# Halved state and score matmuls in a fused linear-attention and MLP kernel

## The chip, the cores and the metric

The kernel runs on one core of a Trainium2 chip. The metric is the device time of one execution in microseconds (us). The engines are named as the profile names them: PE is TensorE's matmuls and PEld its weight loads, DVE is VectorE, ACT is ScalarE, POOL is GpSimd, SP is the engine whose queue issues most loads.

## The reference

Linear attention with a decay per head, and then an MLP with a snake activation on its output. Shapes: batch 4, 8 heads, 768 positions, head size 64; the MLP goes from 512 to 2048 and back to 512 over 3072 tokens.

```python
for b in range(nb):                          # blocks of 64 positions
    intra = einsum('bhic,bhjc->bhij', qb, kb) * Dmask
    intra = einsum('bhij,bhjd->bhid', intra, vb)
    inter = einsum('bhid,bhde->bhie', qb * lam_pow, kv_state)
    out[:, :, sl] = intra + inter
    kv_state = lam_block * kv_state + einsum('bhsd,bhse->bhde', kb * rev_pow, vb)
x = out.transpose(0, 2, 1, 3).reshape(B * S, H * D)
h = x @ w_in
s = sin(alpha * h)
g = h + s * s / (alpha + 1e-9)
return g @ w_out
```

Inputs and the output are float32; the kernel multiplies in bfloat16 and accumulates in float32.

## The kernel before

The attention works on 24 blocks of 128 positions (4 sequences of 6 blocks each). The decay is put into q and k by a scaling on POOL, so that a block needs four kinds of small matmuls, each with 64 or 128 columns of moving data:

- `part_S` (line 535): the scores of a block, 128 keys by 128 queries, for eight heads. Heads lie two to a column group on partitions 0 to 63 and 64 to 127. Eight matmuls contract over 64 partitions into 128 output partitions (one bank of PSUM for the even heads, one for the odd ones). DVE then multiplies by the causal mask into `Sm`.
- `inter` inside `part_O` (line 601): the state's part of the output for the blocks after number 12 that are not first in their sequence (`wide`). `Zd` holds two heads' states of 64 by 64 as blocks on the diagonal of a tile of 128 by 128, so that one matmul serves two heads; four matmuls do it.
- the rest of `part_O` (line 610): for earlier blocks (`n and not wide`) the state's part as eight matmuls of 64 by 64 with `Zc`, and for all blocks eight matmuls of `v2` with `Sm` (line 623), with 64 output partitions each.
- `part_Z` (line 559): the state's update, eight matmuls with 64 output partitions (line 568).

`run` (line 514) puts such parts into one uninterrupted run of matmuls: first every `inter`, then the parts in the order given. `piece_G(s, t)` is the run of the scores of block s, the output of block t and the state update of block t, where t is mostly s - 1. Only the run's last matmul signals the other engines.

The MLP works on six chunks of 512 tokens. `unit_A` and `unit_A2` (lines 671 and 705) are the first product, followed by sin on ACT, a square on ACT or POOL, and a multiply-add on DVE into `gT`; `unit_B` (line 736) is the second product, and ACT copies its result out (line 749). All of these use the array as one tile of 128 by 128. Chunks 2 to 5 run in a loop that puts one unit_A, sometimes a `piece_G`, and one quarter of a unit_B in turn. So most runs of small matmuls stand between two groups of 128 by 128 matmuls.

The order on every engine comes from a planner (`_Plan`): each operation is given an estimated duration, and the planner lays the operations out by these and sets the semaphores. For the runs, the estimates are numbers in the code: 0.33 for `part_S`, and 0.55 for `part_O` where it is wide.

Of the kernel before, what the change touches and what calls it, by code (L numbers as in the profile page):

```python
# [32 lines left out]
class _Plan:  # L33
# [20 lines left out]
    def op(self, eng, emit, dur, reads=(), writes=(), dma=None, after=(), issue=0.4, lat=2.6, runs=64):  # L54
        o = _Op(eng, emit, dur, tuple(reads), tuple(writes), dma, after, issue, lat, runs)
        for b in o.reads:
            if b in self.writer:
                o.deps.add(self.writer[b])
        for b in o.writes:
            if b in self.writer:  # L60
                o.deps.add(self.writer[b])
            o.deps.update(self.readers.get(b, ()))
        o.deps.update(after)
        for b in o.reads:
            self.readers.setdefault(b, []).append(o)
        for b in o.writes:
            self.writer[b] = o
            self.readers[b] = []
        o.deps.discard(o)
        o.lead = self.lead  # L70
        self.ops.append(o)
        return o
# [171 lines left out]
def bass_lightning_attn__then__act_snake_kernel(  # L244
# [35 lines left out]
    with es:  # L280

        def sb(name, shape, dt):
            return es.enter_context(nc.sbuf_tensor(name, shape, dt))

        def ring(name, n, shape, dt):
            return [sb(f"{name}_{i}", shape, dt) for i in range(n)]
# [17 lines left out]
        qkT = sb("qkT", [128, RT, 8, 128], BF16)  # L304
        Sm = ring("Sm", 2, [128, 8, 128], BF16)
        Zc = ring("Zc", 2, [128, 4, D], BF16)
        Zd = ring("Zd", 2, [128, 4, 128], BF16)
# [17 lines left out]
        ps = [banks[:, 512 * i:512 * i + 512] for i in range(8)]  # L325
# [4 lines left out]
        def _(_unused_eng):  # L330
# [7 lines left out]
            def bank(i):  # L338
                return ("bank", i)
# [195 lines left out]
            def part_S(s, b0, b1):  # L535
                jt, jq, u = s % RT, s % RT // 2 * 2, slice(64 * (s % 2), 64 * (s % 2) + 64)

                def mm(e):
                    ins = None
                    for jp in range(4):  # L540
                        for h in range(2):
                            r = slice(64 * h, 64 * h + 64)
                            ins = e.matmul(  # L543
                                ps[(b0, b1)[h]][:, 128 * jp:128 * (jp + 1)].rearrange("p (t x) -> p t x", x=64),
                                qkT[r, jt, 4 + jp, :], qkT[r, jq:jq + 2, jp, u],
                            )
                    return ins

                assert b1 == b0 + 1

                def then():
                    op("DVE", lambda e: e.tensor_tensor(  # L552
                        Sm[s % 2][:, :, :],
                        banks[:, 512 * b0:512 * b0 + 1024].rearrange("p (c i) -> p c i", i=128),
                        mask[:, :, :], ALU.mult), 1.25, [bank(b0), bank(b1), "mask"], [("Sm", s % 2)])

                return mm, 0.33, [("qT", jq), ("qT", jq + 1), ("kT", jt)], [bank(b0), bank(b1)], then
# [31 lines left out]
            def part_O(s, ob, ob2=None):  # L589
                n, j, jq, u = s % NB, s % R2, s % RT // 2 * 2, slice(64 * (s % 2), 64 * (s % 2) + 64)  # L590
                c, i4 = s // BPC, s % BPC
                obs = [ob, ob] if ob2 is None else [ob, ob2]
                new = (0,) if ob2 is None else (0, 2)
                reads = [("v2", j), ("qT", jq), ("qT", jq + 1), ("Sm", s % 2)]
                wide = n and s > SD
                if wide:
                    reads += [("Zd", (s - 1) % 2, 0), ("Zd", (s - 1) % 2, 1)]
                elif n:
                    reads += [("Zc", (s - 1) % 2)]

                def inter(e):
                    for jp in range(4):
                        ins = e.matmul(  # L603
                            ps[obs[jp // 2]][:, 128 * jp:128 * (jp + 1)].rearrange("p (t x) -> p t x", x=64),
                            Zd[(s - 1) % 2][:, jp, :], qkT[:, jq:jq + 2, jp, u],
                            start=(jp in new), stop=False, skip_group_check=True,
                        )
                    return ins

                def mm(e):  # L610
                    ins = None
                    if n and not wide:
                        for jp in range(4):
                            for h in range(2):
                                r = slice(64 * h, 64 * h + 64)
                                e.matmul(
                                    ps[obs[jp // 2]][r, 128 * jp:128 * (jp + 1)].rearrange("p (t x) -> p t x", x=64),
                                    Zc[(s - 1) % 2][r, jp, :], qkT[r, jq:jq + 2, jp, u],
                                    start=(jp in new), stop=False, skip_group_check=True,
                                )  # L620
                    for jp in range(4):
                        for h in range(2):
                            ins = e.matmul(  # L623
                                ps[obs[jp // 2]][64 * h:64 * h + 64, 128 * jp:128 * (jp + 1)],
                                v2[j][:, 2 * jp + h, :], Sm[s % 2][:, 4 * h + jp, :],
                                start=(n == 0 and jp in new), stop=(jp == 3), skip_group_check=True,
                            )
                    return ins

                def then():  # L630
                  for eng, a0, a1, dur in ((("ACT", 0, 2, 0.45), ("DVE", 2, 4, 0.4)) if ob2 is not None else (((("ACT", 0.73, 0.4), ("DVE", 0.7, 0.0)), 0, 4, 0),)):
                    op(eng, lambda e, a0=a0, a1=a1: (e.copy if e is nc.scalar else e.tensor_copy)(  # L632
                        xT[c % RX][:, a0:a1, BL * i4:BL * (i4 + 1)].rearrange("p a (x t) -> p a t x", t=2),
                        ps[obs[a0 // 2]][:, 128 * a0:128 * a1].rearrange("p (a t x) -> p a t x", t=2, x=64)), dur,
                       [bank(obs[a0 // 2])], [("xT", c % RX, i4, a) for a in range(a0, a1)])

                return mm, (0.55 if wide else 0.68) if n else 0.35, reads, [bank(b) for b in sorted(set(obs))], then, inter if wide else None
# [194 lines left out]
            for i in range(NM):  # L832
                hb = (6, 0, 3, 1, 2, 5)[i % 6] if i < 10 else (3, 0, 1, 2)[i % 4]
                u = unit_A2(0, i // 2 * 2, i % 2, hb) if i < 2 else unit_A(0, i, hb)
# [23 lines left out]
            for i in range(8):  # L858
                unit_A2(1, 2 * i, 1, (5, 6, 4)[(i + 2) % 3])
                for _ in range(2 if i in (0, 4) else 1):  # L860
                    kind, s = pieces.pop(0)
# [68 lines left out]
```

## Time and profile before

| | us |
|---|---|
| median of 3 runs | 223.14 |
| lowest and highest | 222.13, 223.40 |
| the profiled execution's own time | 223.52 |
| its span, first to last instruction | 221.4 |
| PE busy in the span | 208.6 (94%), 1645 matmuls |
| ACT, DVE, POOL busy | 155.9, 122.6, 89.1 |

| small matmuls | tile rows*columns | moving columns | count |
|---|---|---|---|
| scores, line 543 | 64*128 | 128 | 192 |
| wide state part, line 603 | 128*128 | 128 | 40 |
| early state part, line 616 | 64*64 | 128 | 80 |
| weighted values, line 623 | 128*64 | 128 | 192 |
| state update, line 568 | 128*64 | 64 | 160 |

Busy time of PE is taken from modelled ends of matmuls that overlap; the starts are recorded one by one, so this text works with starts. A row of the timeline merges the instructions of one line: its first number is the start of the first, its second the stretch to the modelled end of the last. The granted TensorE clock is 1.000 over the span.

### The profile page before, as it was taken

How to read it: one execution, taken by the hardware profiler on the slowest of the kernel's cores; microseconds unless marked ns; L12 is line 12 of the kernel's file. 1: busy time of each engine (PE TensorE's matmuls, PEld its weight loads, DVE VectorE, ACT ScalarE, POOL GpSimd, SP SyncE). 2: the span in 40 equal slices, each digit the busy share in tenths (PEclk: the TensorE clock that was granted, in tenths of full speed). 3: DMA queues.
4: the chain of work that ended last, by engine and by line, in shares of the span. 5: the costliest groups of instructions: out<-in, count | busy, mean ns of one | idle time of the engine just before them, and what ended most of it. 6: DMA issues, size and time to landing. Idle time of an engine off the chain costs nothing.

```text
span 221.4 us, 4062 instructions
## 1 busy us (share of the span) xinstructions
PE 208.6 (94%) x1645; PEld 110.7 (50%) x1645; DVE 122.6 (55%) x184; ACT 155.9 (70%) x277; POOL 89.1 (40%) x100
## 2 busy tenths in 40 slices
PE   3889987899898999999999999999999999999995
PEld 1446433456575785545445444545545444444444
DVE  4687775354777887667655455645465544445100
ACT  3735994347697997788788887877788677778211
POOL 4386763454978776863576103011001011110100
DMA  5999999999999999999999752110110011101112
GB/s 131 236 232 271 206 214 208 217 235 237 233 245 275 242 191 245 219 254 189 276 240 245 155 112 33 47 50 0 47 50 21 26 47 50 47 0 49 75 70 95
DMA packets 83651, 33.31 MB, mean 150 GB/s; under 512 B 63520, under 2 KB 80688, under 8 KB 83632
## 3 DMA queue, kind: packets, MB, share of 16 engines
q1 hardware_dynamic: 76880, 24.25, 53.6%
q0 software_dynamic: 3696, 3.67, 9.9%
q10 hardware_dynamic: 3056, 5.13, 6.4%
q8 instruction: 13, 0.21, 0.4%
q14 instruction: 6, 0.05, 0.1%
HBM read 27.28 MB, written 6.29 MB: 152 GB/s over the span
## 4 chain that ended last, share of the span: by engine, by line
PE 63%; DMA 24%; POOL 4%; SPq 4%; ACT 2%; DVE 1%; issue 1%
PE bank L736 32%; PE bank L671 24%; DMA k<-in_k_dram 10%; DMA q<-in_q_dram 5%; DMA v<-in_v_dram 4%; DMA w<-in_moe_w_in_dram 4%; SPq L342 4%; PE bank L705 3%; PE bank L623 2%; PE bank L543 2%; POOL qk L471 1%; POOL qk L464 1%; PE bank L603 1%; POOL u L720 1%; DVE gT L723 1%
## 5 line engine op out<-in xcount | busy, mean ns | idle before, releaser
L736 PE MATMUL bank<-w,gT 128*128 128x512 bf16 (+1 forms) x400 | 94.8, 371 | 0.0
L688 DVE SCALAR_TENSOR_TENSOR gT<-u,rinv,bank 128x512 bf16<-128x512 bf16 x74 | 54.6, 746 | 51.7 <-ACT u L685 34.2
L671 PE MATMUL bank<-xT,w 128*128 128x512 bf16 x296 | 74.2, 379 | 0.6 <-DVE gT L688 0.6
L681 ACT ACTIVATE t<-bank,alpha 128x512 bf16<-128x512 f32 x74 | 50.6, 686 | 24.1 <-PE bank L671 24.0
L736 PEld LDWEIGHTS bank<-w,gT 128*128 128x128 bf16 x400 | 37.7, 98 | 39.6
L686 POOL TENSOR_TENSOR u<-t 128x512 bf16<-128x512 bf16 x19 | 19.7, 1040 | 80.7 <-ACT t L681 79.7
L671 PEld LDWEIGHTS bank<-xT,w 128*128 128x128 bf16 x296 | 28.5, 98 | 34.9 <-DVE gT L688 1.1
L685 ACT ACTIVATE u<-t 128x512 bf16<-128x512 bf16 x55 | 34.4, 629 | 1.8 <-DVE gT L723 0.3
L552 DVE TENSOR_TENSOR Sm<-bank,mask 128x1024 bf16<-128x1024 f32 x24 | 29.2, 1222 | 10.3 <-PE bank L568 7.7
L464 POOL TENSOR_TENSOR qk<-q,Lq 128x512 bf16<-128x512 f32 x24 | 24.5, 1044 | 21.7 <-DMA q<-in_q_dram 18.1
L471 POOL TENSOR_TENSOR qk<-k,Lk 128x512 bf16<-128x512 f32 x22 | 22.9, 1044 | 7.2 <-DMA k<-in_k_dram 7.0
L749 ACT COPY osb<-bank 128x512 f32<-128x512 f32 (+1 forms) x25 | 14.2, 569 | 14.8 <-PE bank L736 14.8
L705 PE MATMUL bank<-xT,w 128*128 128x256 bf16 x176 | 22.3, 273 | 2.0 <-DVE gT L723 2.0
L723 DVE SCALAR_TENSOR_TENSOR gT<-u,rinv,bank 128x256 bf16<-128x256 bf16 x44 | 19.1, 476 | 7.2 <-POOL u L720 4.1
L715 ACT ACTIVATE t<-bank,alpha 128x256 bf16<-128x256 f32 x44 | 18.5, 471 | 3.3 <-PE bank L705 3.1
L705 PEld LDWEIGHTS bank<-xT,w 128*128 128x128 bf16 x176 | 16.2, 98 | 5.5 <-DVE gT L723 3.0
L473 ACT CAST v<-v 128x512 bf16<-128x512 f32 x18 | 11.0, 615 | 7.6 <-DMA v<-in_v_dram 7.6
L632 ACT CAST xT<-bank 128x512 bf16<-128x512 f32 (+1 forms) x18 | 12.9, 716 | 2.8 <-PE bank L568 1.6
L720 POOL TENSOR_TENSOR u<-t 128x512 bf16<-128x512 bf16 x11 | 11.3, 1039 | 4.7 <-ACT t L715 4.6
L543 PE MATMUL bank<-qkT 64*128 64x128 bf16 x192 | 9.8, 226 | 0.2 <-DVE qkT L493 0.2
L623 PE MATMUL bank<-Sm,v 128*64 128x128 bf16 x192 | 9.9, 225 | 0.0
L829 PE MATMUL bank<-mask,ident 128*128 128x512 bf16 x12 | 5.7, 564 | 3.7 <-DVE mask L429 3.7
(55 smaller groups left out, 111.4 us busy)
## 6 DMA issues: line engine op xcount, KB each, us to landing
k<-in_k_dram SPq DMA_DIRECT2D x24, 256.0 KB, 5.5
v<-in_v_dram SPq DMA_DIRECT2D x24, 256.0 KB, 5.5
q<-in_q_dram SPq DMA_DIRECT2D x10, 512.0 KB, 5.5
out_dram<-osb ACTq DMA_DIRECT2D x19, 256.0 KB, 2.0
w<-in_moe_w_out_dram POOLq DMA_DIRECT2D x4, 512.0 KB, 13.1
w<-in_moe_w_in_dram POOLq DMA_DIRECT2D x3, 512.0 KB, 9.0
q<-in_q_dram SPq DMA_DIRECT2D x4, 256.0 KB, 4.6
ws<-in_moe_w_in_dram SPq DMA_DIRECT2D x2, 512.0 KB, 5.4
```

Of the source, the lines that this page charges most:

```text
L464: lambda e, a=a: e.tensor_tensor(qk2[:, j:j + 2, 4 * a:4 * a + 4, :], q32[jq][:, 4 * a:4 * a + 4, :, :].rearrange("p h t d -> p t h d"), b ...
L471: lambda e: e.tensor_tensor(qk2[:, j, H:2 * H, :], k32[jl][:, :, :], lk, ALU.mult), 0.7 if s in (0,1) else 1.05,
L552: op("DVE", lambda e: e.tensor_tensor(Sm[s % 2][:, :, :], banks[:, 512 * b0:512 * b0 + 1024].rearrange("p (c i) -> p c i", i=128), mask[:, ...
L671: ins = e.matmul(ps[hb][:, c0:c1], w1[:, kc, 128 * m:128 * (m + 1)], xT[x][:, kc, c0:c1], start=(kc == 0 and c0 == lo), stop=(kc == NKC - ...
L681: op("ACT", lambda e: e.activation(t16[ju][:, w], ps[hb][:, w], ACTF.Sin, scale=alpha[:, m:m + 1]), 0.69 * f, [bank(hb), "alpha"], [("t16" ...
L685: lambda e: (e.activation(u16[ju][:, w], t16[ju][:, w], ACTF.Square) if e is nc.scalar else e.tensor_tensor(u16[ju][:, w], t16[ju][:, w], ...
L686: e.tensor_tensor(u16[ju][:, w], t16[ju][:, w], t16[ju][:, w], ALU.mult)), 0,
L688: op("DVE", lambda e: e.scalar_tensor_tensor(out=gT[g][:, m, w], in0=u16[ju][:, w], scalar=rinv[:, m:m + 1], in1=ps[hb][:, w], op0=ALU.mul ...
L705: ins = e.matmul(ps[hb][:, 256 * i:256 * i + 256], w1[:, kc, 128 * (m + i):128 * (m + i + 1)], xT[x][:, kc, lo:lo + 256], start=(kc == 0 a ...
L715: op("ACT", lambda e, i=i: e.activation(t16[ju][:, 256 * i:256 * i + 256], ps[hb][:, 256 * i:256 * i + 256], ACTF.Sin, scale=alpha[:, m + ...
L723: op("DVE", lambda e, i=i: e.scalar_tensor_tensor(out=gT[g][:, m + i, lo:lo + 256], in0=u16[ju][:, 256 * i:256 * i + 256], scalar=rinv[:, ...
L736: ins = e.matmul(ps[ob][:, w], gT[g][:, m, 128 * s4:128 * (s4 + 1)], w2[:, m, w], start=(m == 0), stop=(m == NM - 1),)
```

## The change

Both edits split the stationary tile (the weights) of a matmul by output partition, and leave the moving data, the arithmetic and the planner's estimates as they are. In `part_S` each matmul with 128 keys becomes two with 64 keys each: one writes output partitions 0 to 63 and the other 64 to 127. In `inter` each matmul with 128 columns of `Zd` becomes two with 64 columns each. There are 192 more matmuls from the first edit and 40 more from the second, each with its weight load.

```diff
                     for jp in range(4):
                         for h in range(2):
                             r = slice(64 * h, 64 * h + 64)
-                            ins = e.matmul(
-                                ps[(b0, b1)[h]][:, 128 * jp:128 * (jp + 1)].rearrange("p (t x) -> p t x", x=64),
-                                qkT[r, jt, 4 + jp, :], qkT[r, jq:jq + 2, jp, u],
-                            )
+                            for o in (0, 64):
+                                ins = e.matmul(
+                                    ps[(b0, b1)[h]][o:o + 64, 128 * jp:128 * (jp + 1)].rearrange("p (t x) -> p t x", x=64),
+                                    qkT[r, jt, 4 + jp, o:o + 64], qkT[r, jq:jq + 2, jp, u],
+                                )
...
                 def inter(e):
                     for jp in range(4):
-                        ins = e.matmul(
-                            ps[obs[jp // 2]][:, 128 * jp:128 * (jp + 1)].rearrange("p (t x) -> p t x", x=64),
-                            Zd[(s - 1) % 2][:, jp, :], qkT[:, jq:jq + 2, jp, u],
-                            start=(jp in new), stop=False, skip_group_check=True,
-                        )
+                        for o in (0, 64):
+                            ins = e.matmul(
+                                ps[obs[jp // 2]][o:o + 64, 128 * jp:128 * (jp + 1)].rearrange("p (t x) -> p t x", x=64),
+                                Zd[(s - 1) % 2][:, jp, o:o + 64], qkT[:, jq:jq + 2, jp, u],
+                                start=(jp in new), stop=False, skip_group_check=True,
+                            )
                     return ins
```

## The prediction

> **What bounds the kernel now.** I read the page's first and fourth parts, then busy time by stretches, then PE's timeline around a few runs of small matmuls, and last who waits for them.
>
> ```profile
> PE 208.6 (94%) x1645; PEld 110.7 (50%) x1645; DVE 122.6 (55%) x184; ACT 155.9 (70%) x277; POOL 89.1 (40%) x100
> PE 63%; DMA 24%; POOL 4%; SPq 4%; ACT 2%; DVE 1%; issue 1%
> ```
>
> The second line is the chain of work that ended last. Its DMA and POOL shares lie in the first 85 us, as the windows show:
>
> ```profile
> core 0: us, PE busy (x) PEld busy (x) DVE busy (x) ACT busy (x) POOL busy (x), PEclk, DMA share, GB/s
> 43.50:85.39 41.89, 39.80 (x476) 26.76 (x477) 29.33 (x53) 31.86 (x69) 30.18 (x32) 1.00 1.08 234
> 85.39:172.90 87.51, 87.44 (x669) 44.26 (x670) 50.79 (x69) 70.92 (x123) 28.36 (x30) 1.00 0.63 135
> 172.90:218.90 46.00, 45.92 (x230) 22.18 (x228) 14.96 (x21) 26.48 (x43) 5.20 (x5) 1.00 0.13 49
> ```
>
> Up to 85.39 us the loads decide (DMA share above 1). From there to the end PE never stops for more than a moment: what PE loses there, the kernel loses. So the change is priced on PE, after 85.39 us. One run of small matmuls there:
>
> ```profile
> 97.78 1.24 PE L736 MATMUL bank<-w,gT 128*128 128x512 bf16 x5
> 98.86 0.39 PE L603 MATMUL bank<-qkT,Zd 128*128 128x128 bf16 x4
> 99.18 0.40 PE L543 MATMUL bank<-qkT 64*128 64x128 bf16 x8
> 99.50 0.41 PE L623 MATMUL bank<-Sm,v 128*64 128x128 bf16 x8
> 99.75 0.29 PE L568 MATMUL bank<-v,qk 128*64 128x64 bf16 x8
> 99.98 1.25 PE L671 MATMUL bank<-xT,w 128*128 128x512 bf16 x5
> ```
>
> The first number is a start, and 64*128 is the tile, rows by columns. Starts one by one (nanosecond digits are from the trace's single instructions): L603 steps by 0.056. L543 and L623 go in pairs on two disjoint tiles, 0.0035 apart, a pair each 0.056. So four steps cost 0.224 whether they hold four full matmuls or eight halves. L603 to L543 takes 0.32, L543 to L623 0.32, L623 to L568 only 0.25. **Where the tile's shape stays (L623 to L568) the next matmul starts 0.053 after the last; where it changes, 0.146 to 0.152 after: PE stops for 0.09 to 0.10.** Entering L603 from L736 costs nothing, as both are 128*128. Leaving L568 costs 0.099. The run has three stops.
>
> Two other places show the shapes that the change will use:
>
> ```profile
> 61.88 1.04 PE L705 MATMUL bank<-xT,w 128*128 128x256 bf16 x8
> 62.85 0.41 PE L616 MATMUL bank<-qkT,Zc 64*64 64x128 bf16 x8
> 63.19 0.41 PE L623 MATMUL bank<-Sm,v 128*64 128x128 bf16 x8
> 63.44 0.29 PE L568 MATMUL bank<-v,qk 128*64 128x64 bf16 x8
> ```
>
> Eight steps of 0.109 end at 62.76, yet L616 starts at 62.85: 0.093 to enter 64*64. L616 to L623 is again 0.146 between starts, so 64*64 and 128*64 do not join. And
>
> ```profile
> 22.73 0.81 PE L671 MATMUL bank<-xT,w 128*128 128x512 bf16 x3
> 23.47 0.32 PE L568 MATMUL bank<-v,qk 128*64 128x64 bf16 x8
> ```
>
> three steps of 0.216 end at 23.38: 0.093 to enter 128*64 from 128*128, too.
>
> **The change part by part.** A wide run that also has scores, 9 in number (starts 98.86, 103.44, 111.47, 118.03, 127.79, 140.06, 149.82, 159.58, 165.88), goes from 128*128, 64*128, 128*64 to 128*64, 64*64, 128*64.
>
> - Entry: inter is no longer of the shape of what precedes it. +0.093 (rows above).
> - Inter: four pairs for four matmuls, at 0.056 a pair as L623. But a new half-column shape begins with a step of 0.080 (L623, L616), so first to last start is 0.195 against L603's 0.168: +0.027.
> - Inter to scores: a change before and after; 0.152 becomes 0.146, by L616 to L623 the other way: -0.006.
> - Scores: four groups of four on four disjoint quarters. No row shows four at once. Lower bound: 0.056 a group plus the slow first step, 0.195 plus 0.007 for two more issues, against L543's 0.181: +0.021. A gain is excluded: 64*128 pairs already fill the array. Upper bound: two at a time, eight steps, +0.224 more. I take the lower, nearest to two rows: pairs in either direction (64*128 by rows, 128*64 by columns) overlap fully. On pace, L568 starts eight matmuls, each with its load, 0.0157 apart; a group of four at 0.056 needs 0.014. If 0.0157 is the fastest, sixteen take 0.251, +0.027 a score block, or 0.3 over twelve; this goes into the range.
> - Scores to weighted values: 0.146 by L616 to L623, 0.146 before. Exit unchanged.
>
> Sum: 0.093 + 0.027 - 0.006 + 0.021 = 0.135, and the run grows from 1.117 to 1.25. Nine make 1.22.
>
> The Trainium skill bears on the group of four. Its page "TensorE: Matmul & The Clock Gate", Part 3, gives one matmul's time plus about 4 ns per further tile for disjoint tiles, and the lower bound is that (here 0.0035 per pair). The same page, in "Wait — 56ns, not 53.3ns?", has starts never closer than about 25 ns; L568's 0.0157 speaks against its holding across tiles. The sums by these two are 1.2 and, below, 3.2.
>
> The last wide run (172.19) has no scores: L603 to L623 stopped PE before (0.149), after the edit both are 128*64 and join, while the entry now stops: 0.
>
> Runs after 85.39 with scores but no wide inter (87.25, 92.01, 134.07): entry 0.093 for 0.096, scores +0.021: +0.018 each, 0.05.
>
> Runs before 85.39: four (47.15, 70.93, 76.41, 80.50) have scores followed by L616. These become one shape, so a stop of 0.09 and one slow first step go: about -0.10 each. The others gain 0.02. I cost them at nothing but one: the chain passes there through loads of k, v and q, POOL's scaling and one score block (L543 at 44.83, +0.02). If that cover is gone, all four savings count: -0.38.
>
> One stop absorbs some of it:
>
> ```profile
> 112.93 0.71 ACT L632 CAST xT<-bank 128x512 bf16<-128x512 f32 x1
> 113.70 0.33 PEld L671 LDWEIGHTS bank<-xT,w 128*128 128x128 bf16 x3 [0.56 <-ACT xT L632]
> ```
>
> After the run at 111.47 PE waits for ACT's copy: 113.249 to 113.700 between starts, 0.235 over a step of 0.216. The copy itself waits for ACT's square, not for the run's end (112.66 before, 112.80 after, the copy starts at 112.93). So this run's 0.135 is hidden; 0.10 of the wait stays.
>
> No wait is added; a run still signals at its last matmul. That signal comes 0.135 later, to DVE's mask, which has some 5 us until its scores are used, and to ACT's copies, which are needed late elsewhere (the copy of 141.51 serves a chunk that starts near 146). Order and estimates stay. The 232 extra loads and matmuls queue on PE alone.
>
> **Total:** 1.22 - 0.135 + 0.05 + 0.02 = **+1.16 us**. The profiled execution was 223.52 (span 221.4 and 2.1 around it), so it would be 224.7; against the median 223.14 this gives **224.3**, 0.52% more. About 0.5% (1.12 us) is what a measurement of this kernel can tell from no change, so the sum lies at that edge. The three runs before spread from 222.13 to 223.40: I give this case 223.3 to 225.2, the upper end with the 0.3 of the slower pace.
>
> **The rivals.**
>
> - *The quarters go two at a time.* Each score block grows by 0.224; twelve lie after 85.39, 2.69 in all, and the wait at 113.25 hides 0.10 more: 1.16 + 2.59 = 3.75, 226.9. For it: no row has four tiles at once, and L616 uses only the two quarters on the diagonal. Against: the pairs overlap in both directions. 0.08.
> - *Starts have a floor of 0.025.* Sixteen then take 0.400 instead of 0.224: twelve times 0.176, less 0.10 hidden: +3.2, 226.3. Against: the 0.0157 of L568, and pairs 0.0035 apart. 0.04. (The Trainium skill's page "TensorE: Matmul & The Clock Gate" states this floor.)
> - *Not slower: half-column shapes share their set-up, so that inter, scores and values join without a stop.* In a wide run, entry 0.094, inter 0.195, joint 0.053, scores 0.179, joint 0.053, values 0.171 make 0.745 against 0.842 now. Eight count (the ninth only lengthens its wait for ACT): -0.78; two score blocks followed by values (92.01, 134.07) save 0.10 each: -0.98, 222.2. It decides if the gap from 64*64 to 128*64 falls from 0.146 below about 0.10. Against: L616 to L623, ten times at 0.146, is just that change. 0.04.
> - *The halves act as full tiles* (no change of shape is recorded, inter stays joined to what precedes it): within 0.3 of before. Against: half-column outputs of L568 and L623 are recorded as 128*64. 0.04.
>
> **How the numbers follow.** The forecast has 0.80. Its own range holds 0.92 of it, 0.74; up to 226.4 the range takes in the floor, 0.04, and down to 223.2 half of the case without new shapes, 0.02: 0.80 together. The two-at-a-time case is left out above, the shared set-up below. The forecast's sum is close to the edge, and the cost left at its lower bound (the pace) would push up, so I put two thirds of it, 0.53, on slower and 0.27 on within 0.5%. The first two rivals add 0.12 to slower. The last two go to within 0.5%, except for 0.03 on faster, and a draw of loads before 85 us that is luckier adds 0.01 there (taken from the forecast's share): faster 0.04, same 0.31, slower 0.65.
>
> **What would show it.** Right: L603 as 128*64 with 80 matmuls and L543 as 64*64 with 384; the start of a wide run 0.31 after the last start of a 512-column matmul, no longer 0.216; from inter's first start to the scores' 0.34, from the scores' to L623's 0.35; 1.25 from the first start to the next unit's; the wait at 113.25 down to 0.10; PE's stretch from the first gT-bound unit near 85.4 to the end 1.1 longer. Wrong: scores to L623 at 0.57 (two at a time) or 0.52 (floor); no stop at the entry; a new wait of PE after 85 us; or a first 85 us that moves by more than 0.4, which would mean that the early runs were on the path after all.

## The result and the profile after

| | before | after |
|---|---|---|
| median of 22 runs, us | 223.28 | 224.82 |
| lowest to highest, us | 222.13 to 224.89 | 223.75 to 225.82 |
| profiled execution's own time, us | 223.52 | 225.31 |
| its span, us | 221.4 | 223.2 |
| PE matmuls | 1645 | 1877 |

The ratio is 1.0061, 95% interval 1.0043 to 1.0078: slower by 1.36 us (0.96 to 1.74, of 223.28). The forecast was 224.3 and slower by 1.16.

The page of the kernel after, engine busy times and the chain by engine:

```profile
PE 209.0 (94%) x1877; PEld 110.5 (50%) x1877; DVE 122.5 (55%) x184; ACT 156.1 (70%) x277; POOL 88.9 (40%) x100
PE 64%; DMA 24%; POOL 4%; SPq 4%; ACT 1%; issue 1%; DVE 1%
```

PE has 232 more matmuls, but its busy time rises by only 0.4 us. The change is hard to see here: busy time is built on modelled, overlapping ends. It shows in the starts. Busy time by stretches of the kernel after:

```profile
core 0: us, PE busy (x) PEld busy (x) DVE busy (x) ACT busy (x) POOL busy (x), PEclk, DMA share, GB/s
86.00:174.00 88.00, 88.00 (x788) 43.51 (x788) 50.10 (x69) 70.62 (x122) 28.41 (x30) 1.00 0.65 134
174.00:220.00 46.00, 46.00 (x241) 22.39 (x241) 15.65 (x21) 26.91 (x42) 5.19 (x5) 1.00 0.12 46
```

After 86 us PE still never stops for more than a moment. The granted clock was 0.96 in the first 43.5 us of this execution and 1.00 from there on; in the stretch from 86.6 to 219 us it was 1.00 in every trace of this text. One wide run with scores, PE's timeline:

```profile
98.42 1.24 PE L738 MATMUL bank<-w,gT 128*128 128x512 bf16 x5
99.59 0.41 PE L605 MATMUL bank<-qkT,Zd 128*64 128x128 bf16 x8
99.94 0.42 PE L544 MATMUL bank<-qkT 64*64 64x128 bf16 x16
100.29 0.41 PE L625 MATMUL bank<-Sm,v 128*64 128x128 bf16 x8
100.53 0.29 PE L569 MATMUL bank<-v,qk 128*64 128x64 bf16 x8
100.76 0.61 PE L673 MATMUL bank<-xT,w 128*128 128x512 bf16 x2
```

The state (L605, L603 before) is now 128*64, the scores (L544) 64*64. Five steps of 0.216 from 98.42 end at 99.50, and the state starts at 99.59: the new stop. State to scores takes 0.35, scores to values 0.35; each was 0.32. From first start to the next unit it is 1.163 against 1.117, and the 0.093 of the entry lies ahead of that.

The stage after the loads can be measured by itself, from the first of the sixteen L705 (after: L707) matmuls, which stand behind PE's last wait for gT, to the start of the last matmul. Its begin in the kernel after:

```profile
86.00 1.92 PE L707 MATMUL bank<-xT,w 128*128 128x256 bf16 x16 [1.69 <-DVE gT L725]
```

The last matmul starts at 220.333 (trace; before: 218.550, and the stage begins at 85.391). So the stage takes 134.335 after and 133.159 before, **+1.18 us**. The other 0.61 between the two spans lies ahead of the stage; in the experiments this part differs from trace to trace without following the edits.

### The profile page after: what moved, and what is told of

The parts are those of the page before. It is cut to its first block, busy times and chain, and to the rows that moved or that the text cites. A ratio compares the mean times of both kernels' runs of the same rounds, so it can differ in the third digit from the quotient of the medians.

```text
span 223.2 us, 4526 instructions
## 1 busy us (share of the span) xinstructions
PE 209.0 (94%) x1877; PEld 110.5 (50%) x1877; DVE 122.5 (55%) x184; ACT 156.1 (70%) x277; POOL 88.9 (40%) x100
## 4 chain that ended last, share of the span: by engine, by line
PE 64%; DMA 24%; POOL 4%; SPq 4%; ACT 1%; issue 1%; DVE 1%
PE bank L738 32%; PE bank L673 23%; DMA k<-in_k_dram 10%; DMA q<-in_q_dram 6%; DMA v<-in_v_dram 4%; DMA w<-in_moe_w_in_dram 4%; SPq L342 4%; PE bank L707 3%; PE bank L544 2%; PE bank L625 2%; PE bank L605 2%; POOL qk L471 1%; POOL u L722 1%; POOL qk L464 1%; DVE gT L725 1%
## 5 line engine op out<-in xcount | busy, mean ns | idle before, releaser
L707 PE MATMUL bank<-xT,w 128*128 128x256 bf16 x176 | 22.3, 273 | 2.8 <-DVE gT L725 2.8
L707 PEld LDWEIGHTS bank<-xT,w 128*128 128x128 bf16 x176 | 16.2, 98 | 6.3 <-DVE gT L725 3.8
L544 PE MATMUL bank<-qkT 64*64 64x128 bf16 x384 | 10.4, 229 | 0.2 <-DVE qkT L493 0.2
L625 PE MATMUL bank<-Sm,v 128*64 128x128 bf16 x192 | 10.1, 228 | 0.0
L544 PEld LDWEIGHTS bank<-qkT 64*64 64x64 bf16 x384 | 6.4, 110 | 5.2 <-DVE qkT L493 2.0
```

The lines of the kernel that those rows point to most:

```text
L544: ins = e.matmul(ps[(b0, b1)[h]][o:o + 64, 128 * jp:128 * (jp + 1)].rearrange("p (t x) -> p t x", x=64), qkT[r, jt, 4 + jp, o:o + 64], qkT ...
L707: ins = e.matmul(ps[hb][:, 256 * i:256 * i + 256], w1[:, kc, 128 * (m + i):128 * (m + i + 1)], xT[x][:, kc, lo:lo + 256], start=(kc == 0 a ...
```

## The experiments

Two words are used throughout: PE *stops* where the next matmul starts 0.09 to 0.10 later than the steady pace would have it, and two blocks of matmuls *join* where it starts at the pace. Theory 1 is the forecast's: PE stops wherever the shape of the tile changes, and the change adds one such place per wide run. Theory 2 is a rival with the same total: 232 more matmuls with their loads, some 0.006 us each. In the table, "stage" is as above, each from one trace; the ratio has its 95% interval, and us are the ratio times the median of before that was taken beside it (223.68 for e1 to e4, 223.20 for e5 to e7, 223.91 for e8 and e9). In the traces of e1 to e4, e8 and e9 some matmul records are missing (a row says x3 where four ran), and only starts that are recorded are used. One trace is enough for the stage: in e3, e6 and e8, which leave it alone by theory 1, it comes out within 0.01 of before. Every interval of the time holds the stage's number.

| kernel | matmuls added | stage, us over before | ratio | us over before |
|---|---|---|---|---|
| the change | 232 | +1.18 | 1.0061 (1.0043 to 1.0078) | +1.36 |
| e1, state halves only | 40 | +0.97 | 1.0066 (1.0030 to 1.0103) | +1.48 |
| e2, score halves only | 192 | +0.20 | 1.0021 (0.9995 to 1.0046) | +0.47 |
| e3, state halves beside the values | 40 | 0.00 | 1.0004 (0.9976 to 1.0031) | +0.09 |
| e4, whole state there | 0 | +0.84 | 1.0043 (1.0023 to 1.0064) | +0.96 |
| e5, both halves, state there | 232 | +0.20 | 1.0029 (1.0006 to 1.0051) | +0.65 |
| e6, score halves in four early runs | 32 | 0.00 | 0.9994 (0.9976 to 1.0012) | -0.13 |
| e7, both halves, scores in two visits | 232 | +2.21 | 1.0111 (1.0078 to 1.0144) | +2.48 |
| e8, scores thrice in four early runs | 64 | -0.01 | 0.9999 (0.9973 to 1.0025) | -0.02 |
| e9, scores thrice in four late runs | 64 | +1.80 | 1.0076 (1.0049 to 1.0102) | +1.70 |

**e1 and e2: each edit alone.** e1 is the second hunk of the diff, e2 the first.

> Only the wide state matmuls are halved. Theory 1 (a stop at each change of tile shape): a wide run with scores becomes entry 0.093, state 0.195, stop 0.150, scores 0.181, stop 0.146, values 0.195 = 0.960 against 0.842 before, +0.118. Eight count after 85 us (the ninth is hidden by the wait for ACT, the last wide run has no scores and gains nothing): +0.94 us. Theory 2 (a price per added matmul, 232 for the whole change, so about 0.006 us each): 40 more matmuls, +0.2 us, and the state's first matmul follows a 512-column one after 0.216.

> Only the scores are halved. Theory 1: no stop is added in a wide run; scores 0.202 for 0.181, so +0.02 for each of 12 score blocks after 85 us, less the one hidden: +0.20 us. In four runs before 85 us a stop and a slow first step go (-0.10 each); if these were on the path after all, the sum would be -0.2 us. Theory 2 (a price per added matmul): 192 of the 232, +1.1 us.

PE's timeline of e1, then of e2, one wide run each:

```profile
160.64 1.03 PE L672 MATMUL bank<-xT,w 128*128 128x512 bf16 x4
161.59 0.41 PE L604 MATMUL bank<-qkT,Zd 128*64 128x128 bf16 x8
161.94 0.40 PE L543 MATMUL bank<-qkT 64*128 64x128 bf16 x8
162.27 0.41 PE L624 MATMUL bank<-Sm,v 128*64 128x128 bf16 x8
```

```profile
159.23 1.03 PE L672 MATMUL bank<-xT,w 128*128 128x512 bf16 x4
160.10 0.39 PE L604 MATMUL bank<-qkT,Zd 128*128 128x128 bf16 x4
160.41 0.42 PE L544 MATMUL bank<-qkT 64*64 64x128 bf16 x16
160.76 0.41 PE L624 MATMUL bank<-Sm,v 128*64 128x128 bf16 x8
```

In e1 the state starts 0.95 after the first of four steps of 0.216, in e2 0.86 to 0.87: the stop is in e1 alone. In the stage the 40 matmuls cost 0.97, the 192 cost 0.20, both within 0.03 of theory 1's sums and far from theory 2's 0.2 and 1.1. The 0.97 and 0.20 make 1.17, the change's 1.18: the two edits add up, and the state's halves carry five sixths of it.

**e3 and e4: the same matmuls at another place.** `inter` is called behind the scores, just ahead of the weighted values; e3 has the halves, e4 the whole tiles of before, and the scores are whole in both.

```diff
                 def mm(e):
                     ins = None
+                    if wide:
+                        inter(e)
                     if n and not wide:
...
-                return mm, (0.55 if wide else 0.68) if n else 0.35, reads, [bank(b) for b in sorted(set(obs))], then, inter if wide else None
+                return mm, (0.55 if wide else 0.68) if n else 0.35, reads, [bank(b) for b in sorted(set(obs))], then, None
```

> The state matmuls are halved as in the change and put directly ahead of the weighted values, behind the scores, which stay whole. Theory 1: the state now has the shape of the values and joins them: entry 0.096, scores 0.181, stop 0.146, state 0.195, joint 0.053, values 0.171 = 0.842 as before, so 0.0 us although there are 40 more matmuls than before. Theory 2: +0.2 us, like the state halves at the head of the run, and no difference between the two.

> Nothing is halved; the whole state matmuls are put directly ahead of the weighted values, behind the scores. Theory 1: their shape no longer joins what precedes the run: entry 0.096, scores 0.181, stop 0.149, state 0.168, stop 0.149, values 0.195 = 0.938 against 0.842, +0.096 in eight runs: +0.77 us with no matmul added. Theory 2: 0.0 us.

PE's timeline of e3, then of e4:

```profile
159.87 0.40 PE L543 MATMUL bank<-qkT 64*128 64x128 bf16 x8
160.20 0.41 PE L604 MATMUL bank<-qkT,Zd 128*64 128x128 bf16 x8
160.44 0.39 PE L626 MATMUL bank<-Sm,v 128*64 128x128 bf16 x8
160.67 0.29 PE L568 MATMUL bank<-v,qk 128*64 128x64 bf16 x8
```

```profile
160.01 0.40 PE L543 MATMUL bank<-qkT 64*128 64x128 bf16 x8
160.34 0.40 PE L603 MATMUL bank<-qkT,Zd 128*128 128x128 bf16 x4
160.66 0.41 PE L625 MATMUL bank<-Sm,v 128*64 128x128 bf16 x8
160.91 0.29 PE L568 MATMUL bank<-v,qk 128*64 128x64 bf16 x8
```

The halves join the values (0.24 from L604 to L626, no stop), the whole tiles do not (0.32). e3 has all 40 halved matmuls and a stage equal to before's; e4 adds no matmul and costs 0.84. So neither halving nor count is the price, but the shape of the neighbours. e4's 0.84 is 0.07 over the expectation: the first step behind a change into 128*128 is 0.066 and not 0.056, which the sum had left out in eight runs. The Trainium skill has a rule for this: "TensorEngine Tiling (Array Packing)", Key Properties, says that changing the tiling mode, not just the tile, drains the engine. The traces agree on where PE stops and give the size, 0.09 to 0.10 each time; what fills the stop they do not show.

**e5 and e7: all 232 matmuls, in two other orders.** e5 is the change with e3's order. e7 is the change with half of the scores ahead of the state and half behind it (`mm` in `part_S` takes the pairs of heads to do):

```diff
-                    for p in parts:
-                        if len(p) > 5 and p[5] is not None:
-                            p[5](e)
-                    for p in parts:
-                        ins = p[0](e)
+                    state = [p[5] for p in parts if len(p) > 5 and p[5] is not None]
+                    split = bool(state) and len(parts[0]) == 5
+                    if split:
+                        parts[0][0](e, (0, 1))
+                    for inter in state:
+                        inter(e)
+                    for i, p in enumerate(parts):
+                        ins = p[0](e, (2, 3)) if split and i == 0 else p[0](e)
...
-                def mm(e):
+                def mm(e, jps=range(4)):
                     ins = None
-                    for jp in range(4):
+                    for jp in jps:
```

> The whole change, with the state halves moved directly ahead of the weighted values. Theory 1 (a stop at each change of tile shape): entry 0.093, scores 0.202, stop 0.146, state 0.195, joint 0.053, values 0.171 = 0.860 against 0.842 before, +0.018 for each of eight wide runs and three others: +0.20 us after 85 us, so about 1.0 us less than the change costs. Theory 2 (a price per added matmul): as the change, +1.36 us, since all 232 are there.

> The whole change, and in each wide run with scores half of the scores come before the state and half after it: two shape changes more than in the change. Theory 1: entry 0.093, scores 0.091, stop 0.146, state 0.195, stop 0.149, scores 0.091, stop 0.146, values 0.195 = 1.106 against 0.842 before, +0.264 in eight runs, 0.03 from the ninth and 0.05 from the runs without state: +2.2 us after 85 us, with exactly the matmuls of the change. Theory 2: as the change, +1.36 us.

PE's timeline of e7:

```profile
161.49 0.31 PE L547 MATMUL bank<-qkT 64*64 64x128 bf16 x8
161.72 0.41 PE L608 MATMUL bank<-qkT,Zd 128*64 128x128 bf16 x8
162.07 0.31 PE L547 MATMUL bank<-qkT 64*64 64x128 bf16 x8
162.30 0.41 PE L628 MATMUL bank<-Sm,v 128*64 128x128 bf16 x8
```

The scores now pay twice, 0.23 and 0.23 in place of 0.35. One and the same set of matmuls costs the stage 0.20, 1.18 or 2.21 with three (e5), four (the change) or five (e7) stops in a wide run, entry and exit among them: theory 2 is out, and the price goes with the number of stops. (The kernel before has three, too; e5's 0.20 is the longer score block.) e5 still isn't a gain: 0.65 us in time (0.13 to 1.14).

**e6, e8 and e9: do the early savings count?** In four runs before 85 us the scores and the early state matmuls become one shape. Of the kernel after, PE's timeline:

```profile
79.70 0.42 PE L544 MATMUL bank<-qkT 64*64 64x128 bf16 x16
79.95 0.39 PE L618 MATMUL bank<-qkT,Zc 64*64 64x128 bf16 x8
80.27 0.41 PE L625 MATMUL bank<-Sm,v 128*64 128x128 bf16 x8
80.52 0.29 PE L569 MATMUL bank<-v,qk 128*64 128x64 bf16 x8
```

L544 to L618 is 0.25: the stop is gone, the run is 1.042 for 1.139. e6 has only that. In `part_S`:

```diff
-                            ins = e.matmul(
-                                ps[(b0, b1)[h]][:, 128 * jp:128 * (jp + 1)].rearrange("p (t x) -> p t x", x=64),
-                                qkT[r, jt, 4 + jp, :], qkT[r, jq:jq + 2, jp, u],
-                            )
+                            for o, w in ((0, 64), (64, 64)) if s in (5, 9, 10, 11) else ((0, 128),):
+                                ins = e.matmul(
+                                    ps[(b0, b1)[h]][o:o + w, 128 * jp:128 * (jp + 1)].rearrange("p (t x) -> p t x", x=64),
+                                    qkT[r, jt, 4 + jp, o:o + w], qkT[r, jq:jq + 2, jp, u],
+                                )
```

> The scores are halved only in the four runs before 85 us in which the early state matmuls (64 by 64) follow them; all else is as before. In each of them a stop and a slow first step go, -0.10. If loads and POOL cover these runs: 0.0 us. If they lie on the path: -0.4 us.

Measured: -0.13 us (-0.54 to +0.27). This does not tell 0.0 from -0.4. So e8 adds far more work in the same four runs, and e9 adds as much in the stage where PE decides, to show what such work costs there. Of e8:

```diff
-                    for jp in range(4):
+                    for jp in list(range(4)) * (3 if s in (5, 9, 10, 11) else 1):
```

> The kernel before, but the scores of blocks 5, 9, 10 and 11 (the four runs before 85 us in which the change saves a stop) are computed three times over into the same place: 16 more matmuls, 8 more pairs at 0.056 = 0.45 in each run, 1.8 us of PE in all. If loads and POOL cover these runs, as the forecast has it: 0.0 us. If they lie on the path: +1.8 us, and the savings of 0.10 in each of them counted in the change too.

> The same three-fold scores in four wide runs after 85 us (blocks 14, 15, 17 and 18). If PE decides there, all of it goes through: +1.8 us. If something else had slack to give, less.

PE's timeline of e8:

```profile
76.50 0.84 PE L543 MATMUL bank<-qkT 64*128 64x128 bf16 x24
77.28 0.41 PE L616 MATMUL bank<-qkT,Zc 64*64 64x128 bf16 x8
```

From the scores to the next block it takes 0.78 for 0.32, in four runs, 1.8 us of PE. Early it moves the time by -0.02 (-0.60 to +0.56); late the same work costs 1.70 (1.10 to 2.28), and 1.80 in the stage. So the early runs are covered: by the interval's upper end at most a third of the added work comes through, and a saving of four times 0.10 there is worth at most 0.13. That the loads are what covers them is only read from the chain of the kernel before, which from 47.55 to 84.44 us goes through loads of v and q, the work of ACT, DVE and POOL behind them and 5.4 us of PE, none of it in the four runs; no run changed the loads.

What is left is where the stage begins: 85.39 before, 86.00 after, and in e1 to e9 86.58, 85.75, 85.58, 85.09, 86.02, 85.27, 85.53, 86.03, 86.47. The five kernels with the early joints (after, e2, e5, e6, e7) have a mean of 85.71, the other six 85.86. The begin moves by up to 1.5 us, and in these eleven traces, one for each kernel, not with the edits.

## Why the prediction was right

- *PE after 85 us sets the end.* Right: the stage's +1.18 is nearly the whole of the measured 1.36 (0.96 to 1.74), and e9 shows that PE's work there goes through in full. The parts of it add up: eight wide runs at 0.139, 0.008 left of the ninth and three score blocks at 0.018 make 1.17, so no new wait of PE is in it.
- *Entry +0.093.* Right: the state starts 0.309 after the last 512-column matmul in all ten wide runs, 0.216 plus 0.093.
- *State +0.027.* Right: 0.195 from first to last start.
- *State to scores -0.006.* Half as much: 0.149, taken from the 0.146 of 64*64 to 128*64; the reverse change is 0.003 dearer.
- *Scores +0.021, with four quarters at once.* Right: 0.2015 from first to last start, so sixteen matmuls start 0.0134 apart on average. That was the forecast's open choice, and both rivals on it fall: two at a time would have been 0.42, a floor of 0.025 would have been 0.375. The floor is from the Trainium skill, "TensorE: Matmul & The Clock Gate", section "Wait — 56ns, not 53.3ns?"; it does not hold between disjoint tiles here, while the same page's Part 3 (about 4 ns per further tile) does.
- *A wide run +0.135, nine of them 1.22.* 0.139 each. One slip: the list of signs gave 1.25 from the run's first start to the next unit; that sum holds the entry, which lies ahead of the first start. The stretch named is 1.163.
- *The last wide run 0.* Right. PE's timeline of the kernel after:

```profile
174.06 0.41 PE L605 MATMUL bank<-qkT,Zd 128*64 128x128 bf16 x8
174.31 0.39 PE L625 MATMUL bank<-Sm,v 128*64 128x128 bf16 x8
```

  State and values join (0.25), 0.570 and an entry of 0.093 make 0.663 against 0.664.
- *ACT's copy hides one run.* Right: the wait for the copy fell from 0.235 to 0.104 over a step. The copy still follows ACT's square, 0.54 after the square's start in both kernels (112.39 to 112.93 before). In the kernel after:

```profile
113.31 0.63 ACT L687 ACTIVATE u<-t 128x512 bf16<-128x512 bf16 x1
113.85 0.72 ACT L634 CAST xT<-bank 128x512 bf16<-128x512 f32 x1
114.62 0.55 PEld L673 LDWEIGHTS bank<-xT,w 128*128 128x128 bf16 x4 [0.43 <-ACT xT L634]
```

- *Early runs at nothing, but one score block at 0.02.* The nothing is right, by e8. No run takes the 0.02 by itself; the chain has that block at 0.33 before and 0.35 after (L543, L544).
- *The rival of a shared set-up among half-column shapes* falls: 64*64 to 128*64 is still 0.146 wherever it stands (L544 to L625, twelve times). That of halves acting as full tiles falls, too: L605 is recorded as 128*64, and PE stops ahead of it.
- *The sum.* 1.14 for the stage, 1.18 measured. The median came out 0.5 over the forecast: 0.14 of it is that 22 runs of before have a median of 223.28 and not 223.14, 0.04 the stage; the other 0.3 is no larger than what the begin of the stage moves from trace to trace, but nothing here takes it apart. So the stage bears the sum out to 0.04; that the median, too, fell into the range is in part luck, as single executions lie between 223.75 and 225.82 and the range ended at 225.2.

No order tried beats the kernel before: e3 cannot be told from it, and e4, e5 and e7 are slower. The kernel before already orders its whole state tile beside the 128*128 units, where it joins for free.

## What to carry to other kernels

Price a tile split of small matmuls by the shapes that stand next to it: count the changes of shape along PE's order before and after, at 0.10 to 0.12 us each here, the slow first step behind it included (e4 0.105, e1 0.122, e7 over the change 0.124, in each wide run), and hold the matmul count for nearly free as long as the pieces lie on disjoint tiles. Read this from starts, since busy time hides it (PE busy rose by 0.4 us where the stage lost 1.2). A small saving counts only in the stage whose engine decides; if its size is below the noise, test the stage with added work whose size isn't.

## What the runs showed of the hardware that was not expected

The first step after a stop is slower by an amount that depends on the shape entered: 0.066 into 128*128 (e4) and 0.080 into 128*64 (the change's state) against 0.056 in a steady stream; in 64*64 with four quarters it is 0.080, too, and the whole block of four steps takes 0.2015 from first to last start. The slow first step does not need a change of shape: in the kernel before, L506 (128*128) starts at 51.71, 0.246 after a 512-column matmul of its own shape where the pace is 0.216, and its first step is 0.066 as well (0.056 at 73.82, where it joins).

At a stop the weight load is late together with the matmul. Weight loads and matmuls of the wide run at 111.47 of the kernel before, and of the same run after:

```profile
111.26 0.43 PEld L603 LDWEIGHTS bank<-qkT,Zd 128*128 128x128 bf16 x4
111.47 0.39 PE L603 MATMUL bank<-qkT,Zd 128*128 128x128 bf16 x4
```

```profile
112.49 0.25 PEld L605 LDWEIGHTS bank<-qkT,Zd 128*64 128x64 bf16 x8 [0.42 <-issue]
112.49 0.41 PE L605 MATMUL bank<-qkT,Zd 128*64 128x128 bf16 x8
```

Where the state joins what precedes it, its first load starts 0.21 ahead of its first matmul; where it stops, both start at once. No run tells whether the late load is a part of the stop's cause or only goes with it.

Two blocks of 64*64 with different operands and different quarters join at 0.046 between starts, as do 128*64 blocks at 0.053.
